# Attention computed transposed into a dense feed-forward, with the engines' order written out by hand

## The chip, the cores and the metric

One core of one Trainium2 chip runs the kernel. The metric is the device time of one execution in microseconds (us). The core has a matrix engine (PE, with its weight loads PEld), a vector engine (DVE), a scalar or activation engine (ACT), a general engine (POOL) and a queue engine (SP); 16 DMA engines move data between the chip's memory and the on-chip buffer SBUF. PE writes into PSUM, whose banks hold 512 f32 columns for 128 partitions each.

## The reference

```python
q, k, v: (8, 8, 576, 64) f32        # batch, heads, sequence, head size
kv  = einsum('bhsd,bhse->bhde', k, v)
out = einsum('bhsd,bhde->bhse', q, kv)
rms = sqrt(mean(out * out, axis=-1) + 1e-6)
a   = out / rms * g_norm
x   = a.transpose(0, 2, 1, 3).reshape(4608, 512)
h   = x @ w_in                      # (512, 2048)
g   = h * (1 / (1 + exp(-1.702 * h)))
y   = g @ w_out                     # (2048, 512), result (4608, 512) f32
```

There is no softmax: attention is a 64 x 64 matrix per head, then a product with q, a norm over the 64 values of each head and token, and a two-layer feed-forward over all 4608 tokens.

## The kernel before, in words

Attention goes batch by batch (`emit_attention`, L84 to L213), the feed-forward token chunk by token chunk (`emit_moe`, L215 to L246), nine chunks of 512 tokens. The program emits all eight batches first and then all nine chunks (L248 to L251); a scheduler orders the engines' instructions by this order and by priorities (`tc.high_priority`), so that pieces of both run mixed.

Loads: q, k and v come through POOL's queue (L93), which turns f32 into f16 on the way. A partition receives 64 values (256 bytes read) from each of 36 blocks of 128 rows. The first batch comes in four parts, and the weights `w_in` (L101) and `w_out` (L106) follow batch 1 on the same queue.

Attention for a pair of heads: q is transposed on PE in ten pieces (L123) because a head's 576 rows do not fill blocks of 128, and copied out by DVE (L135); k times v is accumulated in ten pieces (L143) and copied into a block-diagonal 128 x 128 tile (L152 to L154). For each of five token blocks (four of 128, one of 64) the product with q is made with the tokens on the partitions (L165), copied by ACT (L173), squared and summed by DVE (L174, L177). Ln and Exp on ACT turn the sums into the inverse root (L184, L186). DVE multiplies by it and by g_norm (L190, L197), PE transposes the result (L202), and ACT and DVE copy it into `xT` (L211, L213), where the feed-forward reads it with the model dimension on the partitions.

Feed-forward for a chunk: 16 groups of four matmuls of 512 columns (L220) give hT; ACT forms the sigmoid into a tile `sig` (L229) and DVE multiplies it with hT into gT (L232). The two PSUM buffers of hT come free only after that. Then four output tiles of 16 matmuls each (L236), each copied by ACT (L245) and stored by SP, 256 KB at a time (L246).

Of the kernel before, what the change touches and what calls it, by code (L numbers as in the profile page):

```python
# [8 lines left out]
F16 = mybir.dt.float16  # L10
# [3 lines left out]
AXL = mybir.AxisListType  # L14

HIGH = 1 << 20
# [3 lines left out]
def kernel(  # L20
# [13 lines left out]
    NTOK = B * S  # L34
    DM = H * D
    DFF = moe_w_in.shape[1]
    P = 128
    NPAIR = H // 2
    SSUB = (S + P - 1) // P
    s_cnt = [min(P, S - j * P) for j in range(SSUB)]  # L40
    HS_BLOCKS = (2 * S) // P
    assert (2 * S) % P == 0

    EPS = 1e-6
    QK_SCALE = 1.702

    N_TCHUNK = NTOK // 512
    FO = DFF // P
    KO = DM // P

    const = ctx.enter_context(tc.tile_pool(name="const", bufs=1))
    dram = ctx.enter_context(tc.tile_pool(name="dram", bufs=1, space=bass.MemoryType.DRAM))

    kv_io = ctx.enter_context(tc.tile_pool(name="kv_io", bufs=2))
    qtp = ctx.enter_context(tc.tile_pool(name="qtp", bufs=8))
    kv2p = ctx.enter_context(tc.tile_pool(name="kv2p", bufs=8))
    attn = ctx.enter_context(tc.tile_pool(name="attn", bufs=2))
    xp = ctx.enter_context(tc.tile_pool(name="xp", bufs=3))
    moe = ctx.enter_context(tc.tile_pool(name="moe", bufs=2))

    ps_kv = ctx.enter_context(tc.tile_pool(name="ps_kv", bufs=1, space=bass.MemoryType.PSUM))
    ps_ao = ctx.enter_context(tc.tile_pool(name="ps_ao", bufs=1, space=bass.MemoryType.PSUM))
    ps_xt = ctx.enter_context(tc.tile_pool(name="ps_xt", bufs=1, space=bass.MemoryType.PSUM))
    ps_qt = ctx.enter_context(tc.tile_pool(name="ps_qt", bufs=1, space=bass.MemoryType.PSUM))
    ps_h = ctx.enter_context(tc.tile_pool(name="ps_h", bufs=2, space=bass.MemoryType.PSUM))
    ps_o = ctx.enter_context(tc.tile_pool(name="ps_o", bufs=2, space=bass.MemoryType.PSUM))

    g_bc = const.tile([P, D], F32)
    nc.gpsimd.dma_start(out=g_bc, in_=g_norm.unsqueeze(0).broadcast_to([P, D]))
    eps_t = const.tile([P, 1], F32)  # L70
    nc.vector.memset(eps_t, EPS)
    scratch1 = const.tile([P, 1], F32)
    nc.scalar.activation(scratch1, eps_t, AFT.Ln, bias=eps_t, scale=1.0)
    ident = const.tile([P, P], F16)
    make_identity(nc, ident)

    w_in_sb = const.tile([P, KO, DFF], F16)
    w_out_sb = const.tile([P, FO, DM], F16)

    xT_sb = [const.tile([P, NTOK], F16, name=f"xT{i}", tag=f"xT{i}") for i in range(KO)]  # L80

    out_tiled = out.rearrange("(n p) m -> n p m", p=P)

    def emit_attention(b):  # L84
        k_sb = kv_io.tile([P, H * S // P, D], F16, tag="ksb")
        v_sb = kv_io.tile([P, H * S // P, D], F16, tag="vsb")
        q_sb = kv_io.tile([P, H * S // P, D], F16, tag="qsb")
        groups = [[c] for c in range(NPAIR)] if b == 0 else [list(range(NPAIR))]
        for grp in groups:
            c0, c1 = grp[0], grp[-1] + 1  # L90
            hb = c0 * HS_BLOCKS
            for src, dst in ((k, k_sb), (v, v_sb), (q, q_sb)):
                nc.gpsimd.dma_start(  # L93
                    out=dst[:, hb : hb + (c1 - c0) * HS_BLOCKS, :],
                    in_=src[b, 2 * c0 : 2 * c1]
                    .rearrange("h s d -> (h s) d")
                    .rearrange("(hsc sp) d -> sp hsc d", sp=P),
                )
        if b == 1:
            for ko in range(KO):  # L100
                nc.gpsimd.dma_start(  # L101
                    out=w_in_sb[:, ko, :],
                    in_=moe_w_in[ko * P : (ko + 1) * P, :],
                )
            for fq in range(4):
                nc.gpsimd.dma_start(  # L106
                    out=w_out_sb[:, fq * 4 : (fq + 1) * 4, :],
                    in_=moe_w_out[fq * 4 * P : (fq + 1) * 4 * P, :].rearrange(
                        "(fo ki) n -> ki fo n", ki=P
                    ),  # L110
                )

        qT_all = []
        kv2_all = []
        for c in range(NPAIR):
            qTp = ps_qt.tile([P, S], F16, tag="qTp")
            for hl in range(2):
                scol = 0
                for hsc, p0, p1, _st, _sp in _head_row_segments(
                    hl, S, P, c * HS_BLOCKS  # L120
                ):
                    n = p1 - p0
                    nc.tensor.matmul(  # L123
                        qTp[hl * D : hl * D + D, scol : scol + n],
                        q_sb[p0:p1, hsc, :],
                        ident[p0:p1, p0:p1],
                        is_transpose=True,
                        start=True,
                        stop=True,
                        skip_group_check=True,  # L130
                    )
                    scol += n
            with tc.high_priority(offset=HIGH):
                qT = qtp.tile([P, S], F16, tag="qT")
                nc.vector.tensor_copy(qT, qTp)  # L135
            qT_all.append(qT)

            kvp = ps_kv.tile([P, D], F32, tag="kvp")
            base_hsc = c * HS_BLOCKS
            for hl in range(2):  # L140
                segs = _head_row_segments(hl, S, P, base_hsc)
                for hsc, p0, p1, start, stop in segs:
                    nc.tensor.matmul(  # L143
                        kvp[hl * D : hl * D + D, :],
                        k_sb[p0:p1, hsc, :],
                        v_sb[p0:p1, hsc, :],
                        start=start,
                        stop=stop,
                    )
            with tc.high_priority(offset=HIGH):  # L150
                kv2 = kv2p.tile([P, P], F16, tag="kv2")
                nc.vector.memset(kv2, 0.0)  # L152
                nc.vector.tensor_copy(kv2[0:D, 0:D], kvp[0:D, :])
                nc.vector.tensor_copy(kv2[D:P, D:P], kvp[D:P, :])  # L154
            kv2_all.append(kv2)

        rsn = attn.tile([P, SSUB, H], F32, tag="rsn")
        nc.vector.memset(rsn, 0.0)
        aos = attn.tile([P, SSUB, 4 * P], F16, tag="aos")
        sqb = attn.tile([P, SSUB, 4 * P], F16, tag="sqb")  # L160
        for j in range(SSUB):
            cnt = s_cnt[j]
            ao = ps_ao.tile([P, 4 * P], F32, tag="ao")
            for c in range(NPAIR):
                nc.tensor.matmul(  # L165
                    ao[0:cnt, c * P : (c + 1) * P],
                    qT_all[c][:, j * P : j * P + cnt],
                    kv2_all[c],
                    start=(c == 0),
                    stop=(c == NPAIR - 1),  # L170
                )
            with tc.high_priority(offset=HIGH):
                nc.scalar.copy(aos[0:cnt, j, :], ao[0:cnt, :])  # L173
            nc.vector.tensor_mul(  # L174
                sqb[0:cnt, j, :], aos[0:cnt, j, :], aos[0:cnt, j, :]
            )
            nc.vector.reduce_sum(  # L177
                rsn[0:cnt, j, :],
                sqb[0:cnt, j, :].rearrange("p (h e) -> p h e", e=D),
                axis=AXL.X,  # L180
            )

        lnm = attn.tile([P, SSUB, H], F32, tag="lnm")
        nc.scalar.activation(lnm, rsn, AFT.Ln, bias=eps_t, scale=1.0 / D)  # L184
        rstd = attn.tile([P, SSUB, H], F32, tag="rstd")
        nc.scalar.activation(rstd, lnm, AFT.Exp, bias=0.0, scale=-0.5)  # L186
        wb = attn.tile([P, SSUB, H, D], F16, tag="wb")
        for j in range(SSUB):
            cnt = s_cnt[j]
            nc.vector.tensor_tensor(  # L190
                wb[:, j, :, :],
                rstd[:, j, :].unsqueeze(2).broadcast_to([P, H, D]),
                g_bc.unsqueeze(1).broadcast_to([P, H, D]),
                op=ALU.mult,
            )
            xsb = xp.tile([P, 4 * P], F16, tag="xsb")
            nc.vector.tensor_tensor(  # L197
                xsb[0:cnt, :], aos[0:cnt, j, :], wb[0:cnt, j, :, :], op=ALU.mult
            )
            xtp = ps_xt.tile([P, KO, P], F16, tag="xtp")  # L200
            for ko in range(KO):
                nc.tensor.transpose(  # L202
                    xtp[:, ko, 0:cnt],
                    xsb[0:cnt, ko * P : (ko + 1) * P],
                    ident[0:cnt, 0:cnt],
                )
            with tc.high_priority(offset=HIGH // 2):
                for ko in range(KO):
                    dst = xT_sb[ko][:, b * S + j * P : b * S + j * P + cnt]
# [38 lines left out]
    for b in range(B):  # L248
        emit_attention(b)
# [49 lines left out]
```

## Time and profile before

| | |
|---|---|
| Runs (three) | 380.19, 380.15, 380.0 us; median 380.15 |
| Profiled execution: span from first to last instruction | 378.7 us |
| Profiled execution: time around the span | not given; the median of the runs stands 1.45 us above the span |
| PE / DVE / ACT / POOL busy | 341.4 / 217.7 / 183.3 / 56.4 us |
| Matmuls | 2112 |
| Granted PE clock, mean | 0.995 |
| Moved by DMA (as landed) | 28.16 MB, mean 74 GB/s |

How to read the profile: "busy" is the time in which an engine had an instruction under way. A group row names the line, the engine, the operation, written tile <- read tiles, the shapes and the count; behind the bar stand total busy time, mean nanoseconds of one, and the idle time just before them with what ended it. A timeline row has start and length in us. Matmuls are pipelined, so the length of one (0.38 us at 512 columns) is more than the distance between two; distances are taken from start to start. Bytes of the f32-to-f16 loads are counted as landed, half of what is read. A few matmul records can be missing.

### The profile page before, as it was taken

Reading aid. Unit: us, or ns where it says so; the run is one execution under the profiler, and the core shown is the slowest. Engines: PE = TensorE matmul, PEld = TensorE weight load, DVE = VectorE, ACT = ScalarE, POOL = GpSimd, SP = SyncE. Lnnn points to the kernel's source line nnn. Section 1 sums busy time; section 2 is a strip of 40 time slices with the busy share of each in tenths; the row PEclk is TensorE's granted clock in tenths of the full one; section 3 lists DMA queues with packets and bytes.
Section 4 is the critical chain, followed back from the end, with each engine's and each line's share of the span. In section 5 each row is a group of like instructions: output and inputs, shape, how many; then the busy total and the mean of one; then the engine's idle time right before and its main releaser. Section 6 shows DMA issues by size and latency. Waiting matters only on the chain.

```text
span 378.7 us, 5449 instructions
## 1 busy us (share of the span) xinstructions
PE 341.4 (90%) x2112; PEld 167.5 (44%) x2112; DVE 217.7 (58%) x521; ACT 183.3 (48%) x345; POOL 56.4 (15%) x48
## 2 busy tenths in 40 slices
PE   1738878999999999978898999999999999999995
PEld 1526424555555555533443444444444444444442
DVE  1267656768777897899887643532532532531540
ACT  1032384445254767396887643533533443443541
POOL 8944214352531000000000000000000000000000
PEclk9999989999999999999999999999999999999999
DMA  9999999999999301100020011011011011002002
GB/s 73 140 156 208 204 167 147 147 146 160 174 177 155 13 0 57 54 5 0 2 83 28 2 56 56 2 55 55 2 55 55 2 51 60 3 35 75 2 28 83
DMA packets 119049, 28.16 MB, mean 74 GB/s; under 512 B 111840, under 2 KB 113888, under 8 KB 119024
## 3 DMA queue, kind: packets, MB, share of 16 engines
q0 software_dynamic: 113840, 18.39, 86.2%
q1 hardware_dynamic: 5184, 9.44, 6.8%
q8 instruction: 16, 0.26, 0.3%
q14 instruction: 9, 0.07, 0.1%
HBM read 36.73 MB, written 9.44 MB: 122 GB/s over the span
## 4 chain that ended last, share of the span: by engine, by line
PE 71%; DMA 9%; DVE 7%; ACT 6%; POOL 4%; issue 2%; POOLq 0%; ACTq 0%
PE o L236 30%; PE hT L220 28%; DMA v_sb<-in_v_dram 9%; PE qTp L123 6%; PE kvp L143 4%; ACT sig L229 2%; POOL k_sb L93 2%; DVE wb L190 2%; PE xtp L202 2%; PE ao L165 2%; DVE gT L232 2%; POOL q_sb L93 1%; POOL v_sb L93 1%; ACT aos L173 1%; ACT L184 1%
## 5 line engine op out<-in xcount | busy, mean ns | idle before, releaser
L220 PE MATMUL hT<-xT,w_in_sb 128*128 128x512 f16 x576 | 152.5, 384 | 9.0 <-DVE gT L232 9.0
L232 DVE TENSOR_TENSOR gT<-hT,sig 128x512 f16<-128x512 f32 x144 | 98.7, 690 | 94.8 <-ACT sig L229 93.9
L236 PE MATMUL o<-w_out_sb,gT 128*128 128x512 f16 x576 | 148.7, 380 | 0.3 <-ACT osb L245 0.3
L229 ACT ACTIVATE sig<-hT 128x512 f32<-128x512 f32 x144 | 85.4, 597 | 74.7 <-PE hT L220 68.0
L220 PEld LDWEIGHTS <-w_in_sb 128*128 128x128 f16 x576 | 54.1, 98 | 73.4 <-issue 20.4
L236 PEld LDWEIGHTS <-gT 128*128 128x128 f16 x576 | 53.6, 98 | 62.5 <-DVE gT L232 4.3
L245 ACT COPY osb<-o 128x512 f32<-128x512 f32 x36 | 21.0, 585 | 45.9 <-PE o L236 45.1
L173 ACT CAST aos<-ao 128x512 f16<-128x512 f32 (+1 forms) x40 | 23.4, 584 | 32.3 <-PE ao L165 30.1
L143 PE MATMUL kvp<-v_sb,k_sb 128*64 128x64 f16 (+1 forms) x320 | 25.6, 214 | 12.7 <-DMA v_sb<-in_v_dram 11.4
L211 ACT COPY xT<-xtp 128x128 f16<-128x128 f16 (+1 forms) x80 | 20.5, 256 | 33.2 <-PE xtp L202 27.0
L123 PE MATMUL qTp<-ident,q_sb 128*64 128x128 f16 (+1 forms) x320 | 33.7, 243 | 1.7 <-DVE qT L135 0.9
L123 PEld LDWEIGHTS <-q_sb 128*64 128x64 f16 (+1 forms) x320 | 22.1, 118 | 16.0 <-issue 10.0
L143 PEld LDWEIGHTS <-k_sb 128*64 128x64 f16 (+1 forms) x320 | 18.6, 117 | 22.1 <-issue 11.7
L165 PE MATMUL ao<-kv,qT 128*128 128x128 f16 (+1 forms) x160 | 20.2, 239 | 8.8 <-ACT aos L173 5.9
L190 DVE TENSOR_TENSOR wb<-rstd,g_bc 128x512 f16<-128x512 f32 x40 | 26.7, 683 | 2.3 <-ACT rstd L186 2.3
L177 DVE TENSOR_REDUCE rsn<-sqb 128x8 f32<-128x512 f16 (+1 forms) x40 | 26.5, 675 | 0.3
L135 DVE COPY qT<-qTp 128x576 f16<-128x576 f16 x32 | 14.6, 458 | 17.1 <-PE qTp L123 16.9
L165 PEld LDWEIGHTS <-qT 128*128 128x128 f16 (+1 forms) x160 | 12.9, 107 | 21.8 <-issue 13.5
L93 POOL DMA_DIRECT2D k_sb<-in_k_dram x11 | 16.9, 1539 | 32.3 <-PE hT L220 17.0
L213 DVE COPY xT<-xtp 128x128 f16<-128x128 f16 (+1 forms) x80 | 16.9, 211 | 7.6 <-ACT xT L211 7.1
L93 POOL DMA_DIRECT2D q_sb<-in_q_dram x11 | 16.9, 1540 | 12.1 <-PE kvp L143 4.4
L93 POOL DMA_DIRECT2D v_sb<-in_v_dram x11 | 16.9, 1537 | 7.2 <-issue 7.2
(25 smaller groups left out, 124.4 us busy)
## 6 DMA issues: line engine op xcount, KB each, us to landing
out_dram<-osb SPq DMA_DIRECT2D x36, 256.0 KB, 2.0
k_sb<-in_k_dram POOLq DMA_DIRECT2D x7, 576.0 KB, 11.7
v_sb<-in_v_dram POOLq DMA_DIRECT2D x7, 576.0 KB, 11.9
q_sb<-in_q_dram POOLq DMA_DIRECT2D x7, 576.0 KB, 12.5
w_in_sb<-in_moe_w_in_dram POOLq DMA_DIRECT2D x4, 512.0 KB, 16.8
w_out_sb<-in_moe_w_out_dram POOLq DMA_DIRECT2D x4, 512.0 KB, 21.0
k_sb<-in_k_dram POOLq DMA_DIRECT2D x4, 144.0 KB, 4.5
v_sb<-in_v_dram POOLq DMA_DIRECT2D x4, 144.0 KB, 4.7
```

The source lines that it names most:

```text
L93: nc.gpsimd.dma_start(out=dst[:, hb : hb + (c1 - c0) * HS_BLOCKS, :], in_=src[b, 2 * c0 : 2 * c1] .rearrange("h s d -> (h s) d") .rearrang ...
L123: nc.tensor.matmul(qTp[hl * D : hl * D + D, scol : scol + n], q_sb[p0:p1, hsc, :], ident[p0:p1, p0:p1], is_transpose=True, start=True, sto ...
L143: nc.tensor.matmul(kvp[hl * D : hl * D + D, :], k_sb[p0:p1, hsc, :], v_sb[p0:p1, hsc, :], start=start, stop=stop,)
L165: nc.tensor.matmul(ao[0:cnt, c * P : (c + 1) * P], qT_all[c][:, j * P : j * P + cnt], kv2_all[c], start=(c == 0), stop=(c == NPAIR - 1),)
L173: nc.scalar.copy(aos[0:cnt, j, :], ao[0:cnt, :])
L177: nc.vector.reduce_sum(rsn[0:cnt, j, :], sqb[0:cnt, j, :].rearrange("p (h e) -> p h e", e=D), axis=AXL.X,)
L190: nc.vector.tensor_tensor(wb[:, j, :, :], rstd[:, j, :].unsqueeze(2).broadcast_to([P, H, D]), g_bc.unsqueeze(1).broadcast_to([P, H, D]), o ...
L220: nc.tensor.matmul(hT, w_in_sb[:, ko, fo * P : (fo + 1) * P], xT_sb[ko][:, t * 512 : (t + 1) * 512], start=(ko == 0), stop=(ko == KO - 1),)
L229: nc.scalar.activation(sig, hT, AFT.Sigmoid, bias=0.0, scale=QK_SCALE)
L232: nc.vector.tensor_tensor(gT[:, fo, :], hT, sig, op=ALU.mult)
L236: nc.tensor.matmul(o, gT[:, fo, mo * P : (mo + 1) * P], w_out_sb[:, fo, :], start=(fo == 0), stop=(fo == FO - 1),)
L245: nc.scalar.copy(osb, o)
```

## The change

The scheduler is switched off (`manual_schedule`): every engine runs its instructions in the order in which the program emits them.

- *Tokens.* Each head's 576 rows are cut into 512 and 64. A partition p takes the four rows 4p to 4p+3 of the 512, so that one load piece is 1 KB, and the output rows are stored in the same order. The 64 remaining rows of all eight batches make a ninth token tile `x_rem`.
- *Loads.* q, k, v arrive as f32 in `stage` (two buffers); DVE casts them to f16 (`casts`; for batch 0 ACT casts q). Batch 0 and batches 2 to 7 are loaded by SP; POOL loads w_in, batch 1 and w_out, behind a one-column copy (`gate`) that reads the end of batch 0's v.
- *Attention.* kv is made with five matmuls per head pair (`kv_unit`), q is transposed in four pieces of 128 and two shared remainders (`q_unit`), and the product is computed as out^T, weights kv and 512 moving columns (`out_unit`, `out_rem`), so that it needs no transpose afterwards. The sums of squares over a head come from a matmul with a block matrix of ones (`ss_unit`), followed by Ln and Exp on whole 512-column tiles and one DVE operation that multiplies by g and the inverse root. A preload names one activation table for Ln and Exp.
- *Gate.* One activation (`Gelu_apprx_sigmoid`) from PSUM to gT replaces sigmoid and multiply; hT has three PSUM buffers.
- *Output.* DVE copies the output tiles; one 1 MB store per stage, and for the last tile two 128 KB stores per 128 tokens.
- *Order.* Attention of batch 0 comes first. Then stage t does the dense work of tile t with the attention of batch t+1 between its matmuls: kv and q units behind hT groups 2 to 9, out units behind groups 11 to 15, ss units between the matmuls of the second product. The casts for the batch after stand in the third output tile.

```diff
+    ctx.enter_context(tc.manual_schedule())
...
+    load_batch(0, 2)
...
+    first_rows = staged[0]
+    casts(0)
+    gate = const.tile([P, 1], F32)
+    nc.gpsimd.tensor_copy(gate, first_rows["v"][:, H - 1, 0:1])
+    for i in range(4):
+        nc.gpsimd.dma_start(
+            out=w_in_sb[:, :, i * SM : (i + 1) * SM],
+            in_=moe_w_in[:, i * SM : (i + 1) * SM].rearrange("(ko ki) f -> ki ko f", ki=P),
+        )
+    load_batch(1, 1, nc.gpsimd)
+    for i in range(4):
+        nc.gpsimd.dma_start(
+            out=w_out_sb[:, 4 * i : 4 * i + 4, :],
...
+        def kv_unit(c):
...
+            for j in range(J):
+                nc.tensor.matmul(
+                    o,
+                    kh[:, c, j, :],
+                    vh[:, 2 * c : 2 * c + 2, j * D : (j + 1) * D],
+                    start=(j == 0),
+                    stop=False,
+                )
+            nc.tensor.matmul(st["kv"][:, c, :], kr[:, c % 2, :], vr[:, c, :], start=False, stop=True)
...
+        def out_unit(c):
+            w = kvb[b % 2][:, c, :]
+            t = ps_a.tile([P, SM], F32, name="outT", tag="att")
+            nc.tensor.matmul(t, w, st["q"][c][:, 0:SM], start=True, stop=True)
+            a = attn.tile([P, SM], F16, name="aos", tag="aos")
+            nc.scalar.copy(a, t)
+            sq = attn.tile([P, SM], F16, name="sq", tag="sq")
+            nc.vector.tensor_mul(sq, a, a)
...
+        def ss_unit(c):
+            if c == 0:
+                nc.scalar.preload_act_table_set("natural_log_exp_and_others")
...
+            nc.tensor.matmul(t[:, 0:n], ones2, sq, start=True, stop=True)
...
+            nc.scalar.activation(ln[:, 0:n], t[:, 0:n], AFT.Ln, bias=eps_t, scale=1.0 / D)
...
+            nc.scalar.activation(rs[:, 0:n], ln[:, 0:n], AFT.Exp, bias=0.0, scale=-0.5)
+            if c < NPAIR:
+                nc.vector.scalar_tensor_tensor(
+                    x[:, c, :], a, g_col, rs, op0=ALU.mult, op1=ALU.mult
+                )
...
-                nc.scalar.activation(
-                    sig, hT, AFT.Sigmoid, bias=0.0, scale=QK_SCALE
-                )
-                nc.vector.tensor_tensor(gT[:, fo, :], hT, sig, op=ALU.mult)
+            nc.scalar.activation(gT[:, fo, :], h, AFT.Gelu_apprx_sigmoid)
+            for u in units1.get(fo, ()):
+                u()
...
+    early, mid, late = attention(0)
+    for u in early + mid + late:
+        u()
+    casts(1)
+    load_batch(2, 1)
+    for t in range(NT):
+        b = t + 1
+        u1, u2 = {}, {}
+        if b < B:
+            early, mid, late = attention(b)
+            for i, u in enumerate(early):
+                u1.setdefault(2 + i, []).append(u)
+            for i, u in enumerate(mid):
+                u1.setdefault(11 + i, []).append(u)
+            for i, u in enumerate(late):
+                u2.setdefault(divmod(2 + 6 * i, FO), []).append(u)
+        if b + 1 < B:
+            u2.setdefault((2, 8), []).append(lambda b=b: casts(b + 1))
+        if b + 2 < B:
+            u2.setdefault((3, 8), []).append(lambda b=b: load_batch(b + 2, 1))
+        dense(t, u1, u2)
```

More of the change, by code (lines that the diff above doesn't have):

```diff
@@ L82 @@
[L82 to L97, printed above, removed]
-                )
[L99 to L103, printed above, removed]
-                )
[L105 to L110, printed above, removed]
-                )
[L113 to L130, printed above, removed]
-                    )
[L132 to L209, printed above, removed]
-                    if ko % 2 == 0:
-                        nc.scalar.copy(dst, xtp[:, ko, 0:cnt])
-                    else:
-                        nc.vector.tensor_copy(dst, xtp[:, ko, 0:cnt])
```

222 lines of the change are left out of this document (162 added, 60 removed).

## The prediction

> **What bounds the kernel now.** I read the page first: busy shares, the slices, the chain.
>
> ```profile
> span 378.7 us, 5449 instructions
> PE 341.4 (90%) x2112; PEld 167.5 (44%) x2112; DVE 217.7 (58%) x521; ACT 183.3 (48%) x345; POOL 56.4 (15%) x48
> ...
> PE   1738878999999999978898999999999999999995
> ...
> GB/s 73 140 156 208 204 167 147 147 146 160 174 177 155 13 0 57 54 5 0 2 83 28 2 56 56 2 55 55 2 55 55 2 51 60 3 35 75 2 28 83
> ...
> PE 71%; DMA 9%; DVE 7%; ACT 6%; POOL 4%; issue 2%; POOLq 0%; ACTq 0%
> ```
>
> PE is 90% busy and holds 71% of the chain, so it looks full. But matmuls overlap, and a busy PE need not be issuing as fast as it can. So I next took start-to-start distances from the timeline, in a quiet stretch: dense first product, dense second product, then the attention's four kinds (in each pair the second row is what started next).
>
> ```profile
> 264.42 1.02 PE L220 MATMUL hT<-xT,w_in_sb 128*128 128x512 f16 x4
> 265.28 0.38 PE L236 MATMUL o<-w_out_sb,gT 128*128 128x512 f16 x1
> ...
> 278.53 9.95 PE L236 MATMUL o<-w_out_sb,gT 128*128 128x512 f16 x45
> ...
> 288.32 1.89 PE L220 MATMUL hT<-xT,w_in_sb 128*128 128x512 f16 x8
> ```
>
> ```profile
> 153.24 0.70 PE L143 MATMUL kvp<-v_sb,k_sb 128*64 128x64 f16 x10
> 153.87 0.61 PE L236 MATMUL o<-w_out_sb,gT 128*128 128x512 f16 x2
> 154.31 0.39 PE L202 MATMUL xtp<-ident,xsb 128*128 128x128 f16 x4
> 154.54 2.10 PE L236 MATMUL o<-w_out_sb,gT 128*128 128x512 f16 x9
> ```
>
> ```profile
> 149.55 0.90 PE L123 MATMUL qTp<-ident,q_sb 128*64 128x128 f16 x10
> 150.38 0.39 PE L236 MATMUL o<-w_out_sb,gT 128*128 128x512 f16 x1
> ```
>
> A 512-column matmul costs 0.86/4 = 0.215 us in one product and 9.79/45 = 0.218 in the other; I use 0.2163. Dense work is 9 stages of 128, 1152 matmuls: 249.2 us. Ten kv matmuls take 0.63 us, ten q transposes 0.83, four 128-column full-array ones 0.23 (0.0575 each; the ao product likewise). Per batch the attention has 40, 40 and 20 + 20 of these: 2.5 + 3.3 + 2.3 = 8.1 us, 65 for eight. PE therefore needs 314 us of the 378.7; some 64 are waits and slow clock. The windows say where:
>
> ```profile
> 51.00:54.00 3.00, 3.00 (x9) 1.10 (x8) 1.34 (x4) 2.31 (x4) 0.00 (x0) 0.54 2.46 157
> 28.00:48.00 20.00, 17.28 (x128) 11.06 (x128) 13.24 (x43) 6.59 (x16) 6.92 (x5) 1.00 1.30 205
> 60.00:125.00 65.00, 64.36 (x601) 35.87 (x601) 49.21 (x142) 28.97 (x60) 25.16 (x14) 1.00 3.36 156
> 250.00:275.00 25.00, 24.45 (x112) 10.61 (x111) 9.01 (x14) 10.06 (x17) 0.00 (x0) 1.00 0.11 43
> ```
>
> Columns are PE, PEld, DVE, ACT, POOL busy, granted clock, DMA share, GB/s landed. Up to 125 us the loads run without pause; from 250 on almost nothing moves and PE runs dense. The kernel is held by its loads first, then by PE.
>
> **The change, part by part.**
>
> *Steady stage.* Dense matmuls stay at 128 a stage. Attention per batch becomes 20 kv matmuls and 18 transposes (all 128 columns on the full array: 38 x 0.0575 = 2.19 us), 8 of 512 columns (1.73), four of 64 (at most 0.23) and one of 256 (0.11): 4.3 us instead of 8.1. Upper bound for the small ones, the q row's 0.083: 5.2. I take 4.3, since the xtp row has the same shape. Seven batches lie inside dense stages: 29.8 us (36.4 at the upper bound).
>
> ```profile
> L232 DVE TENSOR_TENSOR gT<-hT,sig 128x512 f16<-128x512 f32 x144 | 98.7, 690 | 94.8 <-ACT sig L229 93.9
> L229 ACT ACTIVATE sig<-hT 128x512 f32<-128x512 f32 x144 | 85.4, 597 | 74.7 <-PE hT L220 68.0 <-DVE gT L232 4.5 <-DVE xT L213 1.0
> L174 DVE TENSOR_TENSOR sqb<-aos 128x512 f16<-128x512 f16 x32 | 12.6, 411 | 2.4 <-ACT aos L173 2.1
> L173 ACT CAST aos<-ao 128x512 f16<-128x512 f32 x32 | 18.8, 586 | 30.6 <-PE ao L165 28.4 <-DVE xsb L197 2.1
> ```
>
> *One gate activation.* L232 (98.7 us of DVE) goes, and with it the link by which hT's buffer waited for ACT and then DVE. No row has the new activation; I price it like the sigmoid, 0.597, of the same shape, and up to a group's length it would cost nothing. A group of four hT matmuls takes 0.865, so ACT keeps up; in the five groups that also carry an out unit, ACT needs 0.597 + 0.586 = 1.18 against PE's 1.08, a lag of 0.5 us in all, which three hT buffers cover. DVE per stage: casts of 6,912 elements (no row; 0.41 to 0.69 per 512, so 5.5 to 9.3 us), the rest some 12 (five scale operations and four copies at 0.69, squares, q copies), below 22 of 32 us. Nothing of it is waited for, unless the in-order queues fail (rival 3).
>
> *Table loads.* Ln and Exp each load a table now, and the sigmoid another:
>
> ```profile
> L229 ACT ACT_TABLE_LOAD x12 | 15.4, 1283 | 0.6 <-PE hT L220 0.4
> L186 ACT ACT_TABLE_LOAD x8 | 10.3, 1283 | 0.1
> L184 ACT ACT_TABLE_LOAD x7 | 9.0, 1283 | 0.1
> ...
> 202.10 1.28 ACT L229 ACT_TABLE_LOAD   x1
> 203.40 1.08 ACT L229 ACTIVATE sig<-hT 128x512 f32<-128x512 f32 x2
> ```
>
> After: two per batch. The preload sits in the second product, where ACT has slack. The gate's reload is the one that costs: 0.4 us in its row were spent waiting for hT, so it can start as late as the first group's end. Then 1.28 + 0.60 + about 0.2 of handing over = 2.1 us, while PE has two further buffers, 1.73: 0.4 us a stage, seven stages, 2.8 (zero if it loads earlier). The Trainium skill ("ScalarE: Activation LUTs", section "What ACT_TABLE_LOAD costs") adds a drain of about 1.38 us to each switch, 2.66 in all. By it the reload would cost 1.8 us a stage, and the sum would be 9.7 more. The trace disagrees: the activation starts 0.02 us after the load ends.
>
> *Loads.* Here lies the risk. q, k, v arrive as f32 (3.54 MB a batch, both sides), w_in is 4.19 MB read. Order: batch 0 on SP; then w_in, batch 1, w_out on POOL behind the gate; but batch 2 on SP needs only the buffers that the casts of batch 0 free, at about 13 us. It is issued right then and runs beside w_in and batch 1. PE is queued behind that: the first kv unit of batch 1 follows the third hT group of stage 0, and its last matmul needs the last casts of batch 1.
>
> ```profile
> 1.28 0.68 POOL L69 DMA_DIRECT2D g_bc<-in_g_norm_dram  x1 [0.83 <-POOLq L283]
> ...
> q1 hardware_dynamic: 5184, 9.44, 6.8%
> ...
> out_dram<-osb SPq DMA_DIRECT2D x18, 256.0 KB, 2.0
> ```
>
> ```profile
> q0 software_dynamic: 70248, 8.96, 329.6%
> ...
> out_dram<-osb SPq DMA_DIRECT2D x4, 256.0 KB, 5.7
> ```
>
> The first fence is the page and the stores from 225 us on, the second is 60 to 125 us. Stores, f32 on both sides like the new loads, moved 9.44 MB in 6.8% of 378.7 us: 366 GB/s. Beside loads a store needs 5.7 us instead of 2.0, so the queues do share. Bounds: 8.96 MB landed as f16 in 65 us is 276 GB/s read; 205 landed (28 to 48 us) is 410 read. I take 366, the nearest kind. Until batch 1 is there, 3 x 3.54 + 4.19 = 14.81 MB must pass: 40.5 us (36.1 to 53.7). Add 1.3 to the first issue and 1.3 fixed (2.0 less 0.7 of data): landed at 43.1, q's main part 1.1 earlier. Behind q, DVE casts in order q, q, k, k, v (double), q, q at 0.41 and three rests: 4.0 us (6.7 at 0.69). The kv unit runs at 46. This wait covers what comes before it: batch 0 lands at 2.6 + 9.7 + 1.3 = 13.6, its last casts take some 2, kv units, q transposes and their copies 5, out units and their copies 3, and five pairs of Ln and Exp 6, so stage 0 starts near 30 and reaches the kv unit at 33; w_in's first quarter is there long before. If the loads came 13 us sooner, that chain would be next. Later the loads are hidden: 3.54 MB plus 1.05 MB of stores in a 32 us stage are 143 GB/s. w_out, issued last, lands by 46 + 4.19/0.366 or, sharing with batch 3, by 65, and is first read near 61, its last quarter near 64.5: nothing to 1 us, inside the range. The stores, now one of 1 MB a stage on SP, are queued behind a load that waits for buffers freed a stage earlier; their tile is needed again two stages on.
>
> The Trainium skill ("SBUF — State Buffer", section "SBUF: two separate sides") says that DVE's two-port copies, f32 casts among them, keep GpSimd from writing descriptors. By it each of the four w_in issues might wait for one cast, 4 x 0.69 = 2.8 us at most, and the sum would be up to 336. No row here can show it, as no such cast runs now.
>
> *Cold clock.* After an idle PE the trace has 0.54 of the clock for 3 us:
>
> ```profile
> 51.82 1.91 PE L220 MATMUL hT<-xT,w_in_sb 128*128 128x512 f16 x4
> ```
>
> Four matmuls took 1.91 there against 1.02 above. I add 1.5 us once, behind the long wait.
>
> *Tail.*
>
> ```profile
> 374.87 0.58 ACT L245 COPY osb<-o 128x512 f32<-128x512 f32 x1 [2.87 <-PE o L236]
> ```
>
> From here 3.8 us to the end; with DVE's copy and two stores instead of one, and the last matmul's own length, 4.5.
>
> **Sum.** 46 + 1140 x 0.2163 (246.6; 12 are done before) + 29.8 + 1.5 + 2.8 + 4.5 = 331.2 us of span. Before, 380.15 (median) stands 1.45 over its span, so **332.7, say 333 us**. At 410 GB/s 329, at 276 GB/s 346: its own range is 328 to 346.
>
> **Rivals.** *1. Batch 2's load does not hold up the others* (POOL's queue gets most turns): 3.54 MB less, 9.7 us, **323**. For it: beside the stores the loads still landed 156 GB/s. Against: 5.7 us shows SP's transfers getting their share too.
>
> *2. Mild waits*: casts or units come late by 2 us a stage, **347** (3 us: 354). For it: DVE's queue has casts in front of output copies and q copies. Against: each unit stands at least one 0.865 us group behind its producer.
>
> *3. Slower: the hand order makes PE wait at every unit.* 18 units a batch stand in PE's single queue; each may wait for its copy, at the price of this row:
>
> ```profile
> 20.93 0.58 PE L165 MATMUL ao<-kv,qT 128*128 128x128 f16 x4 [0.67 <-ACT aos L173]
> ```
>
> 18 x 7 x 0.67 = 84 us: **417**. It becomes slower than before from (380.15 - 332.7)/126 = 0.38 us a unit. Against it: that row had no dense work in between; here there is.
>
> *4. The preload does not do what it says*, and Ln and Exp go on loading a table each, now five times a batch: ACT's chain is 5 x (2 x 1.283 + 2 x 0.597) = 18.8 us, begins 2 us into a second product of 14.9 and ends with a scale operation, 6.7 late, seven times: 47, **380**, about level. The L184 and L186 rows speak for it, the named joint set against.
>
> *5. The longer table switch* of the page above: 342.
>
> **How the numbers follow.** Forecast 0.55; rival 1 0.14; 2 0.22; 5 0.02; 4 0.04; 3 0.03. The range reaches from rival 1 with faster loads (323 less 4.4, and 1.5 for no cold stretch: 317) to most of rival 2 (352); rivals 3 and 4 and tails of the rest, under 0.2, stay out. Beyond 0.2% (about what a measurement of this kernel can tell from no change): faster 0.94 (all but 3 and most of 4), same 0.01, slower 0.05 (3 and half of 4).
>
> **What would show it.** PE nearly idle from the third hT group to about 46 us, released by casts that waited for DMA, and batch 2's loads landing before batch 1's; then PE without gaps over 0.5 us, stages of 32 us with attention and 27.7 without; a single reload in front of each stage's first gate; GB/s above 300 in the first 45 us, with w_out still coming behind them until some 60. Wrong if the kv unit runs before 38 us, if a stage takes over 34 us, or if table loads number over 20.

## The result and the profile after

| | before | after |
|---|---|---|
| Time, median of four runs (us) | 380.17 (380.0 to 381.39) | 327.95 (327.16 to 328.07) |
| Profiled execution: own time / span (us) | - / 378.7 | 327.94 / 326.2 |
| Matmuls | 2112 | 1560 |
| Granted PE clock, mean | 0.995 | 0.958 |

The ratio after to before is 0.859, with an interval of 0.855 to 0.864. 333.0 had been forecast, with a range of 317 to 352.

The page of after, first its busy times, the slices of PE, of its clock and of the landed data (one slice is 8.2 us), then the chain:

```profile
span 326.2 us, 3985 instructions
PE 291.3 (89%) x1560; PEld 141.2 (43%) x1560; DVE 127.9 (39%) x279; ACT 174.1 (53%) x287; POOL 14.1 (4%) x24
...
PE   0366059999999999999999999999999999999994
...
PEclk9985559999999999999999999999999999999999
...
GB/s 251 247 216 312 388 234 219 366 25 141 381 42 0 183 369 12 0 228 337 4 1 269 295 0 0 131 0 0 33 98 2 0 79 50 2 0 129 2 64 64
...
PE 85%; DMA 10%; POOL 2%; DVE 1%; SPq 1%; issue 0%; DVEq 0%
```

PE is idle or on half clock in slices 4 to 6, and full from then on. So the kernel now has two parts: a start of 45 us that ends with a wait for loads, and 282 us that PE sets. The chain's rows in the stages (start, length) and two rows of the timeline give the lengths:

```profile
75.94 2.59 PE hT L265 x12
99.65 7.99 PE o L279 x37
107.64 2.59 PE hT L265 x12
```

```profile
44.52 0.27 PE L183 MATMUL kvp<-vrem,kr 128*128 128x128 f16 x1 [6.08 <-DVE vrem L136]
...
321.44 0.69 DVE L288 COPY osb<-o 128x512 f32<-128x512 f32 x1 [2.76 <-PE o L279]
```

A dense matmul takes 7.99/37 = 0.2159 us. A stage takes 107.64 - 75.94 = 31.70; without its 128 dense matmuls, 27.64, that leaves 4.06 for the attention of a batch. The sum, in the prediction's terms: 44.5 (to the last matmul of the first kv unit) + 1140 x 0.2159 = 246.1 + 7 x 4.06 = 28.4 + 2.4 for the cold clock (below) + 0 for table reloads + 4.8 from the last output copy (326.2 - 321.44) = 326.2, the span.

Where the 52 us came from: PE needed 314 us before and needs 1152 x 0.2159 + 8 x 4.06 = 281.2 now, 33 less. The waits and slow stretches went from 64.7 to 45.0, 20 less, and what is left of them is the start (40) and the tail (4.8). How the 20 divide between the new load path, the gate and the order was not measured in full: the gate alone gave 7.8 us in the kernel before and the hand order 7 us in this one (both below), and no run has the new loads alone.

### The profile page after: what moved, and what is told of

Its sections match the earlier page's. It is cut to its first block, busy times and chain, and to the rows that moved or that the text cites. A ratio compares the mean times of both kernels' runs of the same rounds, so it can differ in the third digit from the quotient of the medians.

```text
span 326.2 us, 3985 instructions
## 1 busy us (share of the span) xinstructions
PE 291.3 (89%) x1560; PEld 141.2 (43%) x1560; DVE 127.9 (39%) x279; ACT 174.1 (53%) x287; POOL 14.1 (4%) x24
## 4 chain that ended last, share of the span: by engine, by line
PE 85%; DMA 10%; POOL 2%; DVE 1%; SPq 1%; issue 0%; DVEq 0%
PE o L279 38%; PE hT L265 38%; DMA qf<-in_q_dram 8%; DMA vf<-in_v_dram 2%; PE ss L228 2%; PE kvp L176 2%; PE qTp L194 2%; PE outT L204 2%; POOL w_in_sb L149 1%; SPq L68 1%; PE kvp L183 1%; DVE qh L132 0%; POOL kf L68 0%; DVE kh L129 0%; POOL vf L68 0%
## 5 line engine op out<-in xcount | busy, mean ns | idle before, releaser
L272 ACT ACTIVATE gT<-hT 128x512 f16<-128x512 f32 x144 | 86.0, 597 | 118.9 <-PE hT L265 118.7
L265 PE MATMUL hT<-xT,w_in_sb 128*128 128x512 f16 x512 | 130.5, 389 | 2.0 <-DVE xT L234 2.0
L279 PE MATMUL o<-w_out_sb,gT 128*128 128x512 f16 x576 | 131.1, 379 | 0.0
L288 DVE COPY osb<-o 128x512 f32<-128x512 f32 x36 | 24.7, 687 | 56.0 <-PE o L279 56.0
L234 DVE SCALAR_TENSOR_TENSOR xT<-aos,g_col,rs 128x512 f16<-128x512 f16 x32 | 24.0, 749 | 27.2 <-ACT rs L232 27.2
L230 ACT ACTIVATE ln<-ss,eps_t 128x512 f32<-128x512 f32 (+1 forms) x40 | 25.2, 631 | 0.1
L232 ACT ACTIVATE rs<-ln 128x512 f32<-128x512 f32 (+1 forms) x40 | 23.5, 587 | 1.3
L188 DVE CAST kvb<-kvp 64x256 f16<-64x256 f32 x16 | 6.8, 422 | 40.6 <-PE kvp L183 40.5
L198 DVE COPY qT<-qTp 128x512 f16<-128x512 f16 (+1 forms) x32 | 14.6, 458 | 16.0 <-PE qTp L196 9.6
L206 ACT CAST aos<-outT 128x512 f16<-128x512 f32 x32 | 18.4, 580 | 4.1 <-PE outT L204 4.0
L265 PE MATMUL hT<-x_rem,w_in_sb 128*128 128x512 f16 x64 | 14.0, 379 | 0.0
## 6 DMA issues: line engine op xcount, KB each, us to landing
qf<-in_q_dram SPq DMA_DIRECT2D x6, 1024.0 KB, 13.1
```

The source lines that it names most:

```text
L206: nc.scalar.copy(a, t)
L230: nc.scalar.activation(ln[:, 0:n], t[:, 0:n], AFT.Ln, bias=eps_t, scale=1.0 / D)
L232: nc.scalar.activation(rs[:, 0:n], ln[:, 0:n], AFT.Exp, bias=0.0, scale=-0.5)
L234: nc.vector.scalar_tensor_tensor(x[:, c, :], a, g_col, rs, op0=ALU.mult, op1=ALU.mult)
L265: nc.tensor.matmul(h, w_in_sb[:, ko, fo * P : (fo + 1) * P], x[:, ko, :], start=(ko == 0), stop=(ko == KO - 1),)
L272: nc.scalar.activation(gT[:, fo, :], h, AFT.Gelu_apprx_sigmoid)
```

## The experiments

Times are medians; the ratio to the kernel before, with its interval, stands behind each. Differences in us are to after, 327.95, unless another kernel is named.

### The start: four edits, and all together

The timeline of after around the long wait shows what came in which order:

```profile
29.58 1.91 PE L265 MATMUL hT<-xT,w_in_sb 128*128 128x512 f16 x4
...
37.08 0.69 DVE L130 CAST vh<-vf 128x1024 f16<-128x1024 f32 x1 [2.52 <-DMA vf<-in_v_dram]
...
40.80 0.76 DVE L132 CAST qh<-qf 128x512 f16<-128x512 f32 x2 [3.03 <-DMA qf<-in_q_dram]
...
44.19 0.60 DVE L136 CAST vrem<-vrf 64x256 f16<-64x256 f32 x2
```

The third hT group starts at 29.58; then PE stands in its queue in front of the kv unit, whose last matmul needs `vrem`. Its cast ends only when those of q and v that stand in front of it on DVE have run, and q landed at 40.8.

**cast_order.** The q casts go behind those of k, v and the remainders.

```diff
             ev(out=vh[:, 2 * c0 : 2 * c0 + 4, :], in_=src["v"][:, 2 * c0 : 2 * c0 + 4, :])
-            for c in range(c0, c0 + 2):
-                eq(**pair(qh, src["q"], c))
...
+        for c in range(NPAIR):
+            eq(**pair(qh, src["q"], c))
         eq(out=qr, in_=src["qr"].rearrange("p (u l) d -> p u (l d)", l=2))
```

> The changed kernel, with the casts of a batch in the order k, v, remainders, then q. Theory A: the first kv unit of batch 1 waits for its remainder rows, which the POOL queue lands right behind q, at about 42 us of the span; the cast order then gives back only the casts that stood between, 1.5 to 2.5 us: 325.5 to 326.5 us. Theory B: the unit waits because DVE's queue holds q's casts in front; v is there at 37.1 us, so the unit runs near 39.5 and the time falls by some 5 us, to 323.

Measured: 325.48 us (0.854, 0.850 to 0.859), 2.5 less. Its timeline:

```profile
40.61 0.29 DVE L131 CAST kr<-krf 128x256 f16<-128x256 f32 x1 [2.15 <-DMA krf<-in_k_dram]
...
41.34 0.27 PE L183 MATMUL kvp<-vrem,kr 128*128 128x128 f16 x1 [3.70 <-DVE vrem L134]
```

The DVE casts were worth 3.2 us of the wait (44.52 to 41.34), and no more: now the cast of `kr` (k's remainder rows) itself waits for its DMA until 40.6. The small remainder pieces land hardly before q does. The rest of the wait is transfer.

**batch2_later.** Batch 2 is loaded by POOL behind w_out, so that nothing runs beside w_in and batch 1.

```diff
-    load_batch(2, 1)
...
                 "(fo ki) n -> ki fo n", ki=P
             ),
         )
+    load_batch(2, 1, nc.gpsimd)
```

> The changed kernel, with batch 2 loaded by POOL behind w_out instead of by SP at once. Theory A: the two queues share the DMA engines, and some 2.6 MB of batch 2 pass before batch 1 has landed; at 366 GB/s that is 7 us, so the first kv unit of batch 1 runs near 37.5 us and the time is about 321 us. Theory B: POOL's queue was not held up by SP's (the rival of the prediction): no change, 328 us.

Measured: 321.17 us (0.843, 0.838 to 0.848), 6.8 less, and the kv unit at 37.27:

```profile
37.27 0.27 PE L184 MATMUL kvp<-vrem,kr 128*128 128x128 f16 x1 [4.37 <-DVE vrem L136]
```

So the two issuing queues do share the DMA engines, and batch 2's early load cost 7 us. The DMA view of after shows how. First the load of q on each queue, batch 2's on SP and batch 1's on POOL (the last column is us from issue to landing), then the packets and MB of each queue (SP's is q1) from 15 to 41 us:

```profile
qf<-in_q_dram SPq DMA_DIRECT2D x1, 1024.0 KB, 33.4
...
qf<-in_q_dram POOLq DMA_DIRECT2D x1, 1024.0 KB, 24.8
```

```profile
q0 software_dynamic: 2817, 5.31, 77.1%
q1 hardware_dynamic: 2524, 2.47, 32.3%
```

Batch 1's q, issued by POOL at 16.01, landed at 40.8; batch 2's q, issued by SP 1.7 us earlier, landed at 47.7. Up to 41 us only 2.47 MB came through SP's queue, not the 3.54 of batch 2.

**units_later.** In stage 0 alone, the kv and q units of batch 1 stand behind hT groups 8 to 15 instead of 2 to 9, the out units in the second product.

```diff
-                u1.setdefault(2 + i, []).append(u)
+                u1.setdefault((8 if t == 0 else 2) + i, []).append(u)
...
-                u1.setdefault(11 + i, []).append(u)
+                if t == 0:
+                    u2.setdefault((0, 2 + 2 * i), []).append(u)
+                else:
+                    u1.setdefault(11 + i, []).append(u)
...
-                u2.setdefault(divmod(2 + 6 * i, FO), []).append(u)
+                u2.setdefault(divmod((18 if t == 0 else 2) + 6 * i, FO), []).append(u)
```

> The changed kernel, with the kv and q units of batch 1 behind hT groups 8 to 15 of stage 0 instead of 2 to 9 (its out and ss units follow in the second product). No load is touched. Theory A: the wait is only a place in PE's order; six more groups of 0.865 us run during it: 5.2 us less, about 323 us. Theory B: something else of stage 0 waits for the same loads (the weights of the second product, say), and the wait moves: 326 to 328 us.

Measured: 322.26 us (0.845, 0.841 to 0.850), 5.7 less. The unit comes hardly earlier, but six more hT groups lie in front of it, and of the two waits of after (6.3 us for v, 6.1 for `vrem`) one of 5.9 us is left:

```profile
43.74 0.27 PE L183 MATMUL kvp<-vrem,kr 128*128 128x128 f16 x1 [5.93 <-DVE vrem L136]
```

**small_pieces.** A partition takes row 128j + p instead of rows 4p to 4p+3, so that load pieces are 256 bytes instead of 1 KB, in four issues instead of one; the output rows follow.

```diff
-                eng.dma_start(
-                    out=tiles[n][:, 2 * c0 : 2 * (c0 + step), :],
...
+                for j in range(J):
+                    eng.dma_start(
+                        out=tiles[n][:, 2 * c0 : 2 * (c0 + step), j * D : (j + 1) * D],
+                        in_=src[b, 2 * c0 : 2 * (c0 + step), j * P : (j + 1) * P, :].rearrange(
+                            "h p d -> p h d"
+                        ),
+                    )
```

> The changed kernel with row 128j + p of a head in partition p instead of row 4p + j, so that a load piece is 256 bytes instead of 1 KB (four times the issues of a quarter each); the output rows are stored to match. Theory A: small pieces pass at 276 GB/s or less, so batch 1 lands 10 to 15 us later and the first kv unit of batch 1 runs at 55 to 60 us: 338 to 344 us; stages stay at 31.7. Theory B: bytes decide and not pieces: 328 to 331 us.

Measured: 331.77 us (0.872, 0.869 to 0.874), 3.8 more, just above B's range. The kv unit moved by 6.7, to 51.20, but not on theory A's path. It was batch 0 that came late:

```profile
28.33 0.27 PE L184 MATMUL kvp<-vrem,kr 128*128 128x128 f16 x1 [19.33 <-DVE vrem L137]
...
46.79 0.76 DVE L130 CAST kh<-kf 128x512 f16<-128x512 f32 x2
```

Batch 0's first kv unit, at 13.17 in after, waited for its remainder rows until 28.33, and with it all of batch 0's attention. Batch 1's first casts, at 46.79, wait for no DMA: they stand behind batch 0's scale operations on DVE. So A's rate was about right (from 4 to 10 us, when batch 0 loads alone, 226 GB/s landed against 352 in after), and its path was not: once w_in ran beside it (13 to 27 us), SP landed only 0.93 MB and POOL 1.72, and the rest of batch 0 was what came late. The timeline also gives a price for the cold clock. From the kv unit to the fifth hT group behind it:

```profile
51.20 0.22 PE L184 MATMUL kvp<-vrem,kr 128*128 128x128 f16 x1 [1.03 <-DVE vrem L137]
...
55.77 1.03 PE L266 MATMUL hT<-xT,w_in_sb 128*128 128x512 f16 x4
```

And the same stretch of after, from the kv unit to the start of the fifth hT group behind it:

```profile
44.57 1.91 PE L265 MATMUL hT<-xT,w_in_sb 128*128 128x512 f16 x4
...
51.46 1.03 PE L265 MATMUL hT<-xT,w_in_sb 128*128 128x512 f16 x4
```

In small_pieces the wait in front of the unit was 1.0 us and PE came out of it warm (granted clock 1.00 from 51.2 to 55.8): 4.57 us. In after, out of two waits of 6 us, the clock was 0.55 (44.5 to 50) and the same work took 51.46 - 44.52 = 6.94. The difference, 2.4, is the price of the cold clock, and it is what small_pieces got back of its later start: 6.7 - 2.4 = 4.3, as the two spans differ (330.5 and 326.2). Small pieces cost something in the start alone: a stage is 31.70 in its chain too, with four times the issues.

**all_start_edits.** The three edits above that gained, together (units behind groups 6 to 13), with the remainders of batch 1 loaded by SP and the table for Ln and Exp named at the start instead of in front of batch 0's Ln (part of the diff).

```diff
-    load_batch(1, 1, nc.gpsimd)
+    load_batch(1, 1, nc.gpsimd, nc.sync)
...
+    nc.scalar.preload_act_table_set("natural_log_exp_and_others")
     nc.scalar.activation(warm, eps_t, AFT.Ln, bias=eps_t, scale=1.0)
```

> The changed kernel with all edits at the start together: casts in the order k, v, remainders, q; batch 2 loaded by POOL behind w_out; batch 1's remainders loaded by SP; batch 1's kv and q units behind hT groups 6 to 13 of stage 0; the joint table preloaded before the first loads are awaited, so that batch 0 needs no load of it between its copies and Ln. Theory A: PE then waits only for batch 0's own chain (first full hT group near 26 us instead of 27.5) and has no gap behind it: 26 + 249.2 of dense work + 28.5 of attention + 2 cold + 4.8 of tail = 310.5 us of span, 312 us. Theory B: the wait moves to w_out or to batch 1's q, and a part of the 3 single gains is lost: 316 to 320 us.

Measured: 315.41 us (0.828, 0.826 to 0.831), between the theories, 12.5 less than after and the fastest kernel here. The long wait is gone; two short ones remain, and they are 3.1 of the 3.4 us that A had too little:

```profile
35.92 0.22 PE L185 MATMUL kvp<-vrem,kr 128*128 128x128 f16 x1 [1.56 <-DVE vrem L135]
...
50.87 1.67 PE L281 MATMUL o<-w_out_sb,gT 128*128 128x512 f16 x7 [1.55 <-DMA w_out_sb<-in_moe_w_out_dram]
```

### The stages: PE, the gate, the tables, the hand order

**transposes_twice.** Each of the 16 transposes of q per batch is done twice, into the same place.

```diff
-                nc.tensor.transpose(t[:, j * P : (j + 1) * P], qh[:, c, j, :], ident)
+                for _ in range(2):
+                    nc.tensor.transpose(t[:, j * P : (j + 1) * P], qh[:, c, j, :], ident)
```

> The changed kernel, with each of the 16 full q transposes of a batch done twice into the same place (the second overwrites the first with the same values). Theory A: behind the start PE is the bound and has no gaps, so 7 x 16 x 0.0575 = 6.4 us of added PE work appear in full: about 334 us. Theory B: the attention's matmuls run in gaps that PE has anyway: 328 us.

Measured: 333.78 us (0.875, 0.869 to 0.881), 5.8 more. In its chain the stage is 109.33 - 76.73 = 32.60, 0.90 longer: 16 transposes at 0.056 us each.

```profile
76.73 2.59 PE hT L266 x12
...
109.33 2.59 PE hT L266 x12
```

PE work added to a stage lengthens it by its full length. The 33 us counted for removed PE work rest on this by inference; no run takes the new attention out by itself.

**gate_in_two** puts sigmoid and multiply back into after; **gate_alone** puts the single activation into the kernel before.

```diff
-            nc.scalar.activation(gT[:, fo, :], h, AFT.Gelu_apprx_sigmoid)
+            nc.scalar.activation(sig, h, AFT.Sigmoid, bias=0.0, scale=1.702)
+            nc.vector.tensor_tensor(gT[:, fo, :], h, sig, op=ALU.mult)
```

```diff
-                nc.scalar.activation(
-                    sig, hT, AFT.Sigmoid, bias=0.0, scale=QK_SCALE
-                )
-                nc.vector.tensor_tensor(gT[:, fo, :], hT, sig, op=ALU.mult)
+                nc.scalar.activation(gT[:, fo, :], hT, AFT.Gelu_apprx_sigmoid)
```

> The changed kernel with the gate undone: ACT writes the sigmoid to a tile and DVE multiplies it with hT, as before. DVE gets 16 x 0.69 = 11 us a stage more, on top of some 14, within 31.7. Theory A: with three hT buffers and DVE work ordered between the groups it is mostly covered; 0 to 1 us a stage in groups 5 to 15, where DVE needs 1.1 us for a group of 1.09: 328 to 335 us, most likely 331. Theory B: the gate is what made the kernel faster, since hT's buffers waited for ACT and DVE in turn: 10 us or more, over 338 us.

> The kernel before with one part of the change alone: the single gate activation in place of sigmoid and multiply. 98.7 us of DVE work go. Theory A: PE waited 9.0 us for it in all, most of it once a token chunk; 5 to 12 us less, 368 to 375 us. Theory B: DVE was what held the mixed stages, and the gate alone gives most of the gain: under 350 us. Theory C: nothing, since the loads set the pace until 125 us: 380 us.

Measured: gate_in_two 328.69 us (0.864, 0.861 to 0.867; its runs, 327.6 to 330.14, overlap with those of after), gate_alone 372.39 us (0.980, 0.976 to 0.983), 7.8 less than before. The same edit is worth 7.8 us in one kernel and next to nothing in the other. In gate_in_two the stage is 107.30 - 75.60 = 31.70 again, although DVE has 99 us more to do:

```profile
75.60 2.59 PE hT L265 x12
...
107.30 2.59 PE hT L265 x12
```

```profile
L274 DVE TENSOR_TENSOR gT<-hT,sig 128x512 f16<-128x512 f32 x144 | 99.4, 691 | 27.9 <-ACT sig L273 25.4
```

In the kernel before, hT had two buffers and PE waited. There a whole chunk ran from 288.32 to 317.08, 28.76 us, with PE idle in front of its third group; in gate_alone's chain half a chunk takes 13.81 (226.59 - 212.77 = 13.82), 27.6 a chunk:

```profile
290.75 1.02 PE L220 MATMUL hT<-xT,w_in_sb 128*128 128x512 f16 x4 [0.55 <-DVE gT L232]
...
317.08 1.89 PE L220 MATMUL hT<-xT,w_in_sb 128*128 128x512 f16 x8
```

```profile
212.77 13.81 PE o L232 x64
226.59 13.81 PE hT L220 x64
```

That the third buffer is why the edit is worth so little in after is argued from these waits: the two kernels differ in more than the number of buffers, and no run changes that alone.

**no_preload.** The line that names the common table goes; Ln and Exp load a table each, 88 loads in all. **no_preload_scale_late** is the same, but the five scale operations of DVE are emitted behind the third output copy (their inputs get five buffers).

```diff
-            if c == 0:
-                nc.scalar.preload_act_table_set("natural_log_exp_and_others")
```

```diff
-            rs = attn.tile([P, SM], F32, name="rs", tag="rs", bufs=2)
+            rs = attn.tile([P, SM], F32, name="rs", tag="rs", bufs=5)
...
-            if c < NPAIR:
-                nc.vector.scalar_tensor_tensor(
+            st["s"][c] = (a, rs, n)
+        def scale_unit(c):
+            a, rs, n = st["s"][c]
+            if c < NPAIR:
+                nc.vector.scalar_tensor_tensor(
...
+            u2[(3, 15)] = scale
```

> The changed kernel without the line that preloads the joint table: Ln and Exp then load a table each, ten times a batch. Theory A (the rival of the prediction, priced from the trace): a pair on ACT takes 1.24 + 2.57 = 3.8 us, five of them 19 us in a second product of 14.8, and the gate's load comes after that: 4 to 7 us a stage, seven stages, 356 to 377 us, with 360 the likeliest. Theory B: ACT has slack enough, under 335 us.

> The kernel without the preload, with one more edit: the five scale operations of a batch stand on DVE behind the third output copy instead of between the first output copies. The ten table loads a batch stay. Theory A: without the preload 6 of the 10 us a stage were PE waiting for an output buffer, whose copy stood on DVE behind scale operations that waited for ACT; now only the late x is left, 4 to 7 us a stage and some cold clock: 358 to 380 us. Theory B: the table loads themselves make the time: 395 to 400 us as before.

Measured: no_preload 397.69 us (1.046, 1.043 to 1.049), 70 more than after and slower than before: every theory had it too low. A stage is 127.05 - 85.29 = 41.76 in its chain, and the waits name what is late:

```profile
85.29 2.59 PE hT L263 x12
...
127.05 2.59 PE hT L263 x12
```

```profile
PE o L277 <- DVE osb L286: 52.0, 14, 5.9
```

In the timeline ACT works through Ln and Exp with a load in front of each (Ln is shown), and PE waits for an output copy:

```profile
152.64 1.28 ACT L228 ACT_TABLE_LOAD   x1
153.94 0.69 ACT L228 ACTIVATE ln<-ss,eps_t 128x512 f32<-128x512 f32 x1
...
158.01 5.10 PE L277 MATMUL o<-w_out_sb,gT 128*128 128x512 f16 x16 [5.92 <-DVE osb L286]
```

The copy of an output tile stands on DVE behind scale operations that wait for ACT, so the tile's PSUM buffer stays taken and the second product stops. It then restarts cold: its 16 matmuls take 5.10 us here, at a granted clock of 0.70, where 16 warm ones take 3.61 (the tile at 123.43 in the same trace). A stage is 10.06 us longer than in after, and seven of them make the whole 70: 52.0 are waits for output copies, and part of the rest is slow clock behind them. no_preload_scale_late takes the copies out from behind those operations and keeps every table load: 368.65 us (0.967, 0.963 to 0.971). So freeing the copies is worth 29 of the 70 us, and not 52: once they are gone, the next wait shows. What remains, 41 us, is ACT being late. PE waits for xT, whose scale operations need Exp, and for gT, since the gate's activations stand behind the same loads:

```profile
PE hT L267 <- DVE xT L236: 17.4, 22, 3.4
PE hT L267 <- ACT gT L274: 16.1, 7, 2.5
```

Of the 17.4, 8.6 lie in the start, in front of the long wait for loads. That leaves 24.9 us of waits in the stages, of the 41. The mean clock is 0.938 against 0.958; how much of the rest is slow clock behind the waits was not separated.

**scheduler_sqrt.** The hand order is switched off again. The preload goes with it, so Ln and Exp become one Sqrt, and the scale multiplies by the root instead of its inverse.

```diff
-    ctx.enter_context(tc.manual_schedule())
...
-            nc.scalar.activation(ln[:, 0:n], t[:, 0:n], AFT.Ln, bias=eps_t, scale=1.0 / D)
...
-            nc.scalar.activation(rs[:, 0:n], ln[:, 0:n], AFT.Exp, bias=0.0, scale=-0.5)
+            nc.scalar.activation(rs[:, 0:n], t[:, 0:n], AFT.Sqrt, bias=eps_t, scale=1.0 / D)
```

> The changed kernel without the hand order: the scheduler orders the engines from the same emission. Ln and Exp are replaced by one Sqrt activation, so that tables need no preload (two loads a batch, as in the changed kernel); the scale operation then multiplies by the root instead of its inverse, so this is another function, of the same amount of DVE work and 3 us a stage less on ACT, which has slack. Theory A: the gain comes from the work's shape and the order in which it is emitted, not from forbidding the scheduler: 325 to 331 us. Theory B: the hand order is needed to close PE's gaps: over 340 us.

Measured: 334.74 us (0.880, 0.877 to 0.883), 6.8 more than after, between the theories. In its chain the stages are as long as after's, 114.48 - 82.78 = 31.70, and the loss lies ahead of them: the stage that starts at 75.94 in after starts 6.84 later.

```profile
82.78 2.59 PE hT L260 x12
...
114.48 2.59 PE hT L260 x12
```

The timeline shows where:

```profile
44.99 0.26 PE L182 MATMUL kvp<-vrem,kr 128*128 128x128 f16 x1 [5.32 <-DVE vrem L135]
...
53.04 0.76 DVE L131 CAST qh<-qf 128x512 f16<-128x512 f32 x2 [8.10 <-DMA qf<-in_q_dram]
...
54.17 0.26 PE L182 MATMUL kvp<-vrem,kr 128*128 128x128 f16 x1 [7.53 <-DVE vrem L135]
```

The first kv unit of batch 1 is as early as in after (44.99 against 44.52). The third is not: 54.17 against 48.95. The scheduler put casts of batch 2 in front of batch 1's last remainder cast on DVE: the cast at 53.04 waited for batch 2's q, which SP issued at 19.49 and which landed 33.5 us later. PE then worked at a clock of 0.50 until 60 us.

Once the algorithm leaves the stages dense, the scheduler orders them as well as the hand does. The hand order is worth 7 us here, all in the start: it keeps a wait for batch 2 from standing in front of work for batch 1. One Sqrt in place of two activations also shortens ACT's work, so its worth with Ln and Exp may be a little more.

## Why the prediction held, point by point

**The long wait and its length.** Right in place and nearly in size (46 forecast, 44.5 measured), but that the size came so close is luck: two errors cancel. "Until batch 1 is there, 3 x 3.54 + 4.19 = 14.81 MB must pass" was wrong: of batch 2 only k (28.2) and v (40.1) landed before batch 1's q. What passed by 40.8 us was batch 0, w_in, the main part of batch 1 and 2.47 MB of batch 2, 3.54 + 4.19 + 3.15 + 2.47 = 13.35 MB. In the 40.1 us from the first issue (0.74) that is 333 GB/s, not the 366 taken from the stores; some 0.3 MB that landed from behind q on POOL's queue (5.56 MB there in all) would make it 341 to 348. The casts behind q took 3.7 us (4.0 forecast). That batch 2 competes, against rival 1, is shown by batch2_later: its early load cost 7 us, where the rival priced it at 9.7. Its ground, that POOL's queue gets most turns, was half right: the two queues moved about as many packets, and POOL's were larger (last section).

**The stages.** Right: 4.06 us of attention per batch (4.3 forecast), 0.2159 per dense matmul. The lower price for the small matmuls held: transposes_twice measured 0.056 for a transpose of the full array, where the half array's row of before had 0.083.

**The gate.** Right in its price: the new activation takes 0.597 us, and ACT's idle time in front of it is a wait for PE:

```profile
L272 ACT ACTIVATE gT<-hT 128x512 f16<-128x512 f32 x144 | 86.0, 597 | 118.9 <-PE hT L265 118.7
```

**Table loads.** The count was right: 17, two for each of eight batches and one at the start. "The gate's reload is the one that costs" failed, 2.8 forecast and nothing measured. It is the largest part of the 5.0 us that the sum (331.2) had too much. The timeline of after at the end of a stage's last Exp:

```profile
100.40 0.42 ACT L232 ACTIVATE rs<-ln 128x256 f32<-128x256 f32 x1
...
100.84 1.28 ACT L272 ACT_TABLE_LOAD   x1
...
108.54 0.60 ACT L272 ACTIVATE gT<-hT 128x512 f16<-128x512 f32 x1 [6.42 <-PE hT L265]
```

The load runs 0.02 us after Exp, 7.7 us before the gate has its input; it does not wait for the matmul. The 0.4 us in the row of before were read as if it did. Rival 5, the drain that the Trainium skill ("ScalarE: Activation LUTs", section "What ACT_TABLE_LOAD costs") adds to each switch, is not seen here either: also where no_preload loads 88 times, the activation starts 0.02 us behind the load (152.64 + 1.28, then 153.94).

**Cold clock.** Mis-sized: 1.5 forecast from one slow group, 2.4 measured up to the start of the fifth group behind the wait.

**Tail.** 4.8 (4.5 forecast).

**The rivals on the slow side.** Rivals 2 (2 us of waits a stage) and 3 (a wait at every unit) are refuted by the period: with the prices of the matmuls alone a stage was forecast at 27.7 + 4.3 = 32.0, and 31.70 leaves no room for either. Rival 4's condition was made in no_preload, and its price, 380, was too low by 18: it took the late end of ACT's chain alone, and not what stands behind a waiting operation in DVE's queue.

**Fast loads in the first 45 us.** "Above 300 GB/s" was too high as a sign: the slices there show 216 to 388, in part since a load that turns f32 into f16 lands half of what it reads.

## What to carry to other kernels

When an algorithm change leaves PE dense in the stages, look next at the start, where every queue is in order: which transfers are issued in front of the one that PE needs first, and which casts stand in front of the cast that it needs last. An edit's worth depends on what stands around it (the gate was worth 7.8 us in the kernel before, with two hT buffers, and next to nothing in this one, with three), so price it in the kernel that it goes into. Before an operation that may wait is put into an in-order queue, name what is behind it: one such wait blocked output copies, and taking them out from behind it gave back 29 us; another stands where the scheduler's order lost its 7.

## What the runs showed of the hardware

- Two issuing queues shared the DMA engines by packets here, and not by bytes: in 26 us POOL's queue landed 5.31 MB, part of it read at twice that size, in 2817 packets, and SP's 2.47 MB in 2524. From 28 to 36 us, with batch 1 on POOL, it is 731 packets with 2.30 MB against 724 with 0.74 MB (DMA view of that stretch): as many packets, but larger ones. A 1 MB load of SP took 33.4 us there; the median of the six of its kind is 13.1 (page of after).
- A table load did not wait for the input of its activation: it ran 7.7 us ahead of it (100.84, then 108.54).
- POOL's copy of a single column took as long as the DVE cast beside it. Both rows are of after's timeline:

```profile
10.50 0.69 DVE L130 CAST vh<-vf 128x1024 f16<-128x1024 f32 x1 [0.56 <-DMA vf<-in_v_dram]
...
10.53 0.71 POOL L147 COPY gate<-vf 128x1 f32<-128x1 f32 x1 [9.22 <-DMA vf<-in_v_dram]
```

In small_pieces the same copy began at 12.75, inside a pair of DVE casts that ended at 13.13, and took 0.42 us. In both it ends 0.04 to 0.05 us behind the cast beside it. This fits the rule of the Trainium skill ("SBUF — State Buffer", section "SBUF: two separate sides") that such DVE copies hold GpSimd up. What it costs is not shown, as no run has the copy without a cast beside it. POOL's four w_in issues behind it went out in 3.11 us together; the 2.8 us allowed for in the prediction did not come.
- POOL's remainder loads of v and q of batch 1 were issued late, when w_in transfers had landed (waits of 4.0, 3.7 and 3.6 us in after). Those of k were issued without a wait, right behind q (16.88), and still took some 24 us to land: standing in the same queue, the smallest pieces of batch 1 landed no earlier than q. all_start_edits gave them to SP.
